# C v in smaller TensorE tiles, and a new order of the first loads, in a Nystrom attention and feed-forward kernel

## The chip, the cores and the metric

One core of one Trainium2 chip runs the whole kernel. The time is device microseconds of one execution, and the kernels are compared by the median of several executions. The core has a matrix engine (TensorE, PE in the profile, with its weight loads as PEld), a vector engine (DVE), a scalar engine (ACT), GpSimd (POOL) and a queue engine (SP) that issues DMAs. Each engine works through its own instructions in order; POOL and ACT issue some DMAs too.

## The reference

```python
def _attn_ref(q, k, v):                      # 8 batches, 8 heads, 576 rows, 64 columns, float32
    m, scale = 32, 1.0 / np.sqrt(D)
    q_lm = q.reshape(B, H, m, S // m, D).mean(axis=3)
    k_lm = k.reshape(B, H, m, S // m, D).mean(axis=3)
    A = sm(q, k_lm)                          # sm: row softmax of scale * a @ b.T
    Bm = sm(q_lm, k_lm)
    C = sm(q_lm, k)
    Z = Bm.T / (norm1(Bm) * norminf(Bm) + 1e-06)
    for _ in range(6):
        Z = 2 * Z - Z @ Bm @ Z
    return A @ Z @ C @ v

def _moe_ref(x, w1, w2, w3, w_out):          # x: 4608 x 512, the attention's heads side by side
    a = x @ w1                               # w1, w2: 512 x 1024
    b = x @ w2
    h = a * b @ w3                           # w3: 1024 x 1024
    return h @ w_out                         # w_out: 1024 x 512
```

## The kernel before

**How the work is cut.** Four heads of one batch are a quad; there are 16 quads, two to a batch. Two batches are a group, for which the 32x32 inverse is iterated at once; there are four groups. A batch's output is computed in three parts of 192 rows.

**Weights (L312 to L402).** `w3` and `w_out` are multiplied once, into `w34`, because nothing stands between the two products. `w3` comes in eight blocks of 128 rows (512 KB each, tiles `w3n`, a ring of three), is transposed on PE (`w3_tr`, L335), and split into a high and a low fp16 part by ACT (`w3_hi`, L342) and DVE (`w3_lo`, L349), half a block at a time. `w_out` comes in eight blocks (256 KB) and is split likewise (`wout_hi`, L321; `wout_lo`, L326). Each step `mm{j}{c}` is three matmuls of 512 columns. SP issues all of these loads (L309, L316); the first two blocks of `w3` come in two halves. `w_out` lands in the memory of the third and fourth `vb` tile.

**Attention of a quad (L646 to L706).** POOL issues the load of k and q (`lq`, L409), which turns them to fp16 on the way, into one of six `nat` tiles. DVE transposes them (`tk`, `tq`, L438). The means over 18 rows are made by POOL in three steps (`ma`, `mb`, `mc`, L446, L453, L461) for all quads but the first `NE` = 1, for which PE makes them (`M`, L471). PE then computes the scores with the landmarks (`S`, into the tile `wide`) and those of q (`A`); DVE finds maxima and differences (L514, L592, L598), ACT the exponentials (L541, L607), DVE the sums, POOL multiplies (`an`, L620), PE transposes (L629), ACT copies to `aT`.

**C v (L709 to L735).** The exponentials of C, transposed by DVE into `ecT` (L557), are the stationary operand in tiles of 128 rows by 32 columns. The two 64-row halves of a tile belong to two different heads. So that one product over 128 rows does both, each v tile `vb` holds 128 columns for a row, with zeros where row half and head don't match: `const_e` (L292) writes these zeros once on POOL, and a load of v (`load_v`, L414, four DMAs on SP) fills only the other blocks. The sums of the exponentials are masked the same way on POOL (`s_sums`, L546) and multiplied with `unit64`. For a batch this is 36 products of 128 columns and 4 of two columns, into one PSUM bank; DVE divides (`cv_out`, L731, L732).

**The inverse and the dense part.** `norm_mm`, `it_mm` (five rounds), `z_mm` and `w_mm` are small matmuls in 32x32 and 128x64 tiles (L764 to L849). Then, for each batch, `u_mm` (64x32 tiles, 512 columns) folds the inverse and C v into w1 and w2; `d1_mm` multiplies with `aT`; ACT (L954) and DVE (L960) make the product of the two branches, `ab`; `d2_mm` multiplies with `w34`; ACT scales (L986) and SP stores (L1001).

**What sets the order.** Every step is a task with an engine, an expected duration, dependencies, buffers that it takes (`acq`) and gives back (`rel`), a priority and an earliest start (`after`). `Plan.run` (L90) walks through them before the program is built and writes out a fixed order for each engine: of the tasks of an engine that can start soonest, the one with the lowest `prio`, where on PE a task in the tile mode that is set already has a bonus of `MP` = 1.2. The priorities come from `dense(b)` = 66 + 21 b, `att(n)`, `lane(g)` = `dense(2g)` - 16 and `cvt(b)` (L242 to L256). `SLACK` is added to every expected latency. The order that comes out is what each engine executes; nothing is reordered when a load comes late.

**Around the change.** POOL's first tasks are the identity (`cb`, L268), the zeros of the first two `vb` tiles (`ce0`), then the q/k loads; `ce1`, the zeros of the other two, waits for the last `wol` (the last use of `w_out`'s memory). The v loads of quads 0 to 3 wait for `ce0` or `ce1`. Six PSUM banks (`bank`) are shared by all steps.

Of the kernel before, what the change touches and what calls it, by code (L numbers as in the profile page):

```python
# [16 lines left out]
D = 64  # L17
# [3 lines left out]
NC9 = 9  # L21
# [3 lines left out]
MP = 1.2  # L25
# [15 lines left out]
class Plan:  # L41
# [6 lines left out]
    SLACK = 0.05  # L48
# [41 lines left out]
    def run(self):  # L90
# [15 lines left out]
        while len(order) < n:  # L106
            best = None
            for e, cand in avail.items():
                opts = []
                for t in cand:  # L110
                    found = self._slots(t.acq)
                    if found is None:
                        continue
                    at = max(free[e], t.ready, found[0], t.after)
                    opts.append((at, t, found[1]))
                if not opts:
                    continue
                first = min(o[0] for o in opts)
                near = [o for o in opts if o[0] <= first + (0.05 if e == "PE" else 0.0)]
                at, t, got = min(near, key=lambda o: (  # L120
                    o[1].prio - (MP if e == "PE" and o[1].mode == mode else 0.0)))
                if best is None or at < best[0]:
                    best = (at, t, got)
# [41 lines left out]
def kernel(  # L165
# [35 lines left out]
    vbs = slots(fixed, 4, [128, 2, 2, NC9, D], FP32, "vb")  # L201
# [26 lines left out]
    maskS = fixed.tile([128, 2], FP32, name="maskS")  # L228
# [13 lines left out]
    T0 = 66.0  # L242
    PER = 21.0
# [4 lines left out]
    def att(n):  # L248
        first = dense(2 * (n // 4)) - 42.0 + 7.0 * (n % 4)
        return max(0.0 + 6.0 * n, first)  # L250

    def lane(g):
        return dense(2 * g) - 16.0

    def cvt(b):
        return lane(b // 2) - 0.0 + 3.0 * (b % 2)  # L256

    NE = int(1.0)
    L0 = 9.0
    UO = 5.0  # L260
# [10 lines left out]
    def const_c():  # L271
        nc.vector.memset(blockones, 0.0)
        nc.vector.memset(ones, 1.0)
        nc.vector.memset(swapneg, 0.0)
        nc.vector.memset(maskS, 0.0)
        nc.vector.memset(meanS, 0.0)
        for s in range(2):
            nc.vector.memset(maskS[64 * s:64 * s + 64, s:s + 1], 1.0)
        for hh in range(4):
            r = slice(32 * hh, 32 * hh + 32)  # L280
            nc.vector.memset(meanS[r, hh:hh + 1], 1.0 / GRP)
            nc.vector.memset(blockones[r, r], 1.0)
        nc.vector.reduce_sum(out=iden32, in_=ident.rearrange("p (h x) -> p x h", h=4), axis=AX.X)
# [8 lines left out]
    def const_e(i):  # L292
        def fn():
            for t in vbs[2 * i:2 * i + 2]:
                for s in range(2):
                    nc.gpsimd.memset(t[64 * s:64 * s + 64, :, 1 - s, :, :], 0.0)
        return fn
# [5 lines left out]
    add("ce0", "POOL", 4.4, const_e(0), deps=["cb"], prio=-5.0)  # L303
    add("ce1", "POOL", 4.4, const_e(1), deps=[f"wol{c}" for c in range(8)], prio=24.0)
# [7 lines left out]
    def load_w3(j, n):  # L312
        def fn():
            for i in range(n):
                c = slice(DF // n * i, DF // n * i + DF // n)
                nc.sync.dma_start(out=w3n[at(f"w3n{j}")][:, c], in_=moe_w3[128 * j:128 * j + 128, c])  # L316
        return fn
# [12 lines left out]
    def w3_tr(j, h):  # L330
        def fn():
            ps = bank(at(f"ptr{j}{h}"))
            for i in range(4):
                c = 4 * h + i
                nc.tensor.transpose(out=ps[:, 128 * i:128 * i + 128],  # L335
                                    in_=w3n[at(f"w3n{j}")][:, 128 * c:128 * c + 128],
                                    identity=ident[:, :])
        return fn

    def w3_hi(j, h):  # L340
        def fn():
            nc.scalar.activation(out=w3t[at(f"w3t{j}")][:, 0, 512 * h:512 * h + 512],  # L342
                                 in_=bank(at(f"ptr{j}{h}")), func=AXF.Copy, scale=WSC)
        return fn

    def w3_lo(j, h):
        def fn():
            t = w3t[at(f"w3t{j}")]
            nc.vector.scalar_tensor_tensor(  # L349
                out=t[:, 1, 512 * h:512 * h + 512], in0=bank(at(f"ptr{j}{h}")), scalar=WSC,  # L350
                in1=t[:, 0, 512 * h:512 * h + 512], op0=ALU.mult, op1=ALU.subtract)
        return fn
# [17 lines left out]
    def w34_tasks():  # L370
        for j in range(8):
            p0 = 4.0 + 8.0 * j
            n = 2 if j < 2 else 1
            add(f"w3n{j}", "SP", 0.43 * n, load_w3(j, n), acq=[("w3n", f"w3n{j}", 1, 2)],
                prio=p0 - 8.0 if j > 1 else 0.115 * j, after=max(0.0, p0 - 12.0) if j > 1 else 0.0, move=1.46, lat=2.0)
# [8 lines left out]
            for h in range(2):  # L384
                acq = [("P", f"ptr{j}{h}", 1, 2)]
                if h == 0:
                    acq.append(("w3t", f"w3t{j}", 1, 8))
                add(f"tr{j}{h}", "PE", 0.44, w3_tr(j, h),
                    deps=["cb", f"w3n{j}"] + ([f"tr{j}0"] if h else []), acq=acq,
                    rel=[f"w3n{j}"], prio=p0 - 4.0 + h, mode="full")  # L390
                add(f"wh{j}{h}", "ACT", 0.48, w3_hi(j, h), deps=[f"tr{j}{h}"], rel=[f"ptr{j}{h}"],
                    prio=p0 - 3.5 + h)
                add(f"wl{j}{h}", "DVE", 0.61, w3_lo(j, h), deps=[f"tr{j}{h}", f"wh{j}{h}"],
                    rel=[f"ptr{j}{h}"], prio=p0 - 3.5 + h)
            for c in range(8):
                deps = [f"woh{c}", f"wol{c}", f"wh{j}{c // 4}", f"wl{j}{c // 4}"]
# [17 lines left out]
    def load_v(n):  # L414
        def fn():
# [3 lines left out]
            for s in range(2):  # L419
                for t in range(2):  # L420
                    p0 = 64 * s + 32 * t
                    nc.sync.dma_start(out=vb[p0:p0 + 32, :, s, :, :].rearrange("p a c d -> p a (c d)"),
# [123 lines left out]
    def s_sums(n):  # L546
        def fn():
            t = tinies[at(f"mx{n}")]
            nc.gpsimd.tensor_tensor(
                out=t[:, 8:12].rearrange("p (a s) -> p a s", a=2),  # L550
                in0=t[:, 4:6].unsqueeze(2).to_broadcast([128, 2, 2]),
                in1=maskS.unsqueeze(1).to_broadcast([128, 2, 2]), op=ALU.mult)
        return fn

# [91 lines left out]
    def quad_tasks(n):  # L646
        b, qd = divmod(n, 2)
        p = att(n)
        add(f"lq{n}", "POOL", 1.2, load_qk(n), acq=[("nat", f"nat{n}", 1, 3)],
            prio=p - (16.0 if n < 4 else 25.0),  # L650
            after=max(L0, p - (20.0 if n < 4 else 25.0)), move=3.3, lat=2.0)
        add(f"lv{n}", "SP", 1.75, load_v(n), acq=[("vb", f"vb{n}", 1, 1)], deps=[f"ce{n // 2}"] if n < 4 else [],
            prio=cvt(b) - 9.0 + qd, after=max(12.0, cvt(b) - 12.0 + 3 * qd), move=1.65, lat=2.0)
# [38 lines left out]
        add(f"ss{n}", "POOL", 0.2, s_sums(n), deps=[f"se{n}0", f"se{n}1"], prio=p + 2.0)  # L692
# [16 lines left out]
    def cv_mm(b):  # L709
        def fn():  # L710
            ps = bank(at(f"pC{b}"))
            for n in (2 * b, 2 * b + 1):
                qd = n % 2
                sums = tinies[at(f"mx{n}")][:, 8:12].rearrange("p (a s) -> p a s", a=2)
                for hp in range(2):
                    o = 32 * (2 * qd + hp)
                    mm(ps[o:o + 32, 128:130], unit64[:, :], sums[:, hp, :], pos=(0, o))
            for c in range(NC9):
                for n in (2 * b, 2 * b + 1):
                    qd = n % 2  # L720
                    for hp in range(2):
                        o = 32 * (2 * qd + hp)
                        mm(ps[o:o + 32, 0:128], ecTs[at(f"ecT{n}")][:, hp, c, :],
                           vbs[at(f"vb{n}")][:, hp, :, c, :], start=(c == 0), stop=(c == 8), pos=(0, o))
        return fn

    def cv_out(b):
        def fn():
            ps = bank(at(f"pC{b}"))
            rc = tinies[at(f"tc{b}")][:, 0:2]  # L730
            nc.vector.reciprocal(out=rc, in_=ps[:, 128:130])  # L731
            nc.vector.tensor_tensor(out=cvs[at(f"cv{b}")],  # L732
                                    in0=ps[:, 0:128].rearrange("p (s d) -> p s d", s=2),
                                    in1=rc.unsqueeze(2).to_broadcast([128, 2, D]), op=ALU.mult)
# [145 lines left out]
    def cv_tasks(b):  # L880
        n0, n1 = 2 * b, 2 * b + 1
        p = cvt(b)
        add(f"C{b}", "PE", 2.06, cv_mm(b),
            deps=[f"ct{n0}", f"ct{n1}", f"ss{n0}", f"ss{n1}"] + [f"lv{n0}", f"lv{n1}"],
            acq=[("P", f"pC{b}", 1, 1)], rel=[f"ecT{n0}", f"ecT{n1}", f"vb{n0}", f"vb{n1}", f"mx{n0}", f"mx{n1}"],
            prio=p, mode="128x32")
        add(f"co{b}", "DVE", 0.4, cv_out(b), deps=[f"C{b}"],
            acq=[("cv", f"cv{b}", 1, 1), ("tiny", f"tc{b}", 1, 1)],
            rel=[f"pC{b}", f"tc{b}"], prio=p + 2.0)
# [166 lines left out]
    P.ring("w3n", 3)  # L1056
# [5 lines left out]
    for s in range(2):  # L1062
        for qd in range(2):
            for wi in range(2):
                add(f"lw{s}{qd}{wi}", "POOL", 0.62, load_w12(s, qd, wi), prio=dense(0) - 22.0 + qd, after=dense(0) - 26.0,
                    move=0.75, lat=2.0)
# [12 lines left out]
    with tc.manual_schedule():  # L1079
        with tc.tile_pool(name="w34pool", bufs=1) as wp:  # L1080
            w3n = [obig[:, 2 * i:2 * i + 2, :].rearrange("p a x -> p (a x)") for i in range(2)]
            w3n.append(wp.tile([128, DF], FP32, name="w3n2"))
            wof = [vbs[2 + i // 4].rearrange("p a s c d -> p (a s c d)")[:, DM * (i % 4):DM * (i % 4) + DM]
                   for i in range(8)]
# [38 lines left out]
```

## Time and profile before

| | |
|---|---|
| median of 3 runs | 287.32 us (286.81 to 289.51) |
| the profiled execution | 290.63 us, its span 288.9 us |
| TensorE clock granted, mean | 0.992 |
| instructions on PE | 4098 matmuls and transposes, 4098 weight loads |
| DMA | 37.34 MB, mean 129 GB/s |

Busy time of the engines in stretches of the span, in us:

| stretch, us | PE | DVE | ACT | POOL | DMA share |
|---|---|---|---|---|---|
| 0 to 20 | 13.6 | 8.2 | 9.3 | 9.0 | 0.91 |
| 20 to 45 | 21.9 | 16.1 | 8.2 | 20.7 | 0.84 |
| 45 to 60 | 15.0 | 12.9 | 7.8 | 12.9 | 0.59 |
| 60 to 80 | 15.9 | 14.4 | 5.1 | 15.7 | 1.10 |
| 80 to 120 | 39.6 | 35.3 | 28.1 | 32.7 | 0.47 |
| 120 to 160 | 38.3 | 31.9 | 25.0 | 32.9 | 0.66 |
| 160 to 200 | 39.4 | 30.4 | 25.1 | 20.7 | 0.45 |
| 200 to 240 | 39.8 | 29.0 | 25.7 | 4.1 | 0.16 |
| 240 to 289 | 44.3 | 17.9 | 29.7 | 0.0 | 0.22 |

How the lines of the profile are read: in a group or a timeline line stand the line of the program, the engine, the operation, the tiles (out<-in, buffer numbers left out), and the partitions and elements of what is written and read; "x72" is how many there are. "<-" with an engine in a list of waits names what ended a wait; "issue" is time in which the engine waited for nothing that the profile shows. An fp32 matmul stands as two matmuls and two weight loads. All matmuls outside the transposes have the helper's line, L238, so their tiles tell them apart: `vb,ecT` is C v, `tiny,unit` its sums, `xz` the inverse, `bm` its norms, `wo,u` the product of `w3` and `w_out`, `w,wT` the u products, `aT,u` and `w,ab` the dense part, `Tk,lmT` the landmark scores.

### The profile page before, as it was taken

What the parts mean: (1) busy time and instruction counts of PE and PEld (TensorE: products, weight loads), DVE (VectorE), ACT (ScalarE), POOL (GpSimd) and SP (SyncE); (2) the same over time, 40 slices, a digit from 0 to 9 for tenths busy, and PEclk for the clock granted to TensorE, in tenths of its full rate; (3) what the DMA queues carried; (4) which work ended last, traced back from release to release, by engine and by line L of the source; (5) the groups of instructions that cost most, each with busy time, mean ns of one, the idle gap of its engine ahead of it and who ended that gap; (6) DMA issues with size and microseconds to landing.
All of it is one profiled execution on the core that took longest, in us unless ns stands there. A gap on an engine that the chain in (4) does not pass through costs nothing.

```text
span 288.9 us, 9979 instructions
## 1 busy us (share of the span) xinstructions
PE 267.8 (93%) x4098; PEld 176.8 (61%) x4098; DVE 196.0 (68%) x511; ACT 163.9 (57%) x456; POOL 148.9 (52%) x190
## 2 busy tenths in 40 slices
PE   3899699987899999989999999999999999999993
PEld 1446256655456767667667577667657775765762
DVE  0757549897468989956799798587958655443430
ACT  1743236424119798244967953478697454958551
POOL 8239688887897779999488789201111000000000
PEclk9999989999999999999999999999999999999999
DMA  6997982699950197601999816721212102111223
GB/s 196 302 313 183 258 203 75 108 205 263 254 128 2 21 182 148 129 7 39 217 241 217 198 48 178 184 83 40 73 39 76 39 13 68 57 54 52 98 74 109
DMA packets 19181, 37.34 MB, mean 129 GB/s; under 512 B 2880, under 2 KB 3136, under 8 KB 19136
## 3 DMA queue, kind: packets, MB, share of 16 engines
q1 hardware_dynamic: 13136, 24.91, 27.9%
q0 software_dynamic: 5760, 11.54, 23.2%
q8 instruction: 32, 0.52, 0.8%
q10 hardware_dynamic: 240, 0.26, 0.3%
q14 instruction: 13, 0.11, 0.1%
HBM read 38.80 MB, written 9.44 MB: 167 GB/s over the span
## 4 chain that ended last, share of the span: by engine, by line
PE 58%; DVE 18%; DMA 13%; ACT 5%; POOL 3%; issue 2%; SPq 0%; POOLq 0%; ACTq 0%; DVEq 0%
PE bank L238 53%; DMA nat<-in_q_dram 7%; DMA vb<-in_moe_w_out_dram 6%; DVE ab L960 4%; PE wide L238 2%; DVE bank L742 2%; DVE ea L598 2%; ACT u L876 2%; DVE tiny L613 2%; DVE tiny L592 1%; DVE tiny L514 1%; DVE ecT L557 1%; ACT ec L541 1%; POOL ls L453 1%; PE bank L629 1%
## 5 line engine op out<-in xcount | busy, mean ns | idle before, releaser
L238 PEld LDWEIGHTS <-u 128*128 128x128 f16 x960 | 81.4, 100 | 38.1 <-issue 9.4
L960 DVE TENSOR_TENSOR ab<-asb,bank 128x192 f16<-128x192 f16 x192 | 60.2, 346 | 31.7 <-ACT asb L954 30.7
L238 PE MATMUL bank<-aT,u 128*128 128x192 f16 x768 | 80.9, 246 | 0.0
L954 ACT CAST asb<-bank 128x192 f16<-128x192 f32 x192 | 59.0, 352 | 26.1 <-PE bank L238 23.5
L238 PE MATMUL bank<-w,ab 128*128 128x512 f16 (+1 forms) x296 | 73.2, 374 | 0.3
L238 PE MATMUL bank<-wo,u 128*128 128x512 f16 x192 | 52.2, 403 | 3.0 <-ACT u L342 2.6
L453 POOL TENSOR_TENSOR ls<-ls 128x128 f32<-128x128 f32 (+2 forms) x60 | 43.7, 729 | 4.3
L238 PEld LDWEIGHTS <-ab 128*128 128x128 f16 x296 | 27.0, 97 | 23.2 <-issue 5.1
L620 POOL TENSOR_TENSOR ah<-ea,tiny 128x512 f16<-128x512 f32 (+1 forms) x16 | 18.5, 1158 | 42.4 <-DVE tiny L534 24.7
L876 ACT CAST u<-bank 128x512 f16<-128x512 f32 x64 | 34.5, 611 | 5.8 <-PE bank L238 5.0
L446 POOL TENSOR_TENSOR ls<-nat 128x1152 f32<-128x1152 f16 x15 | 35.6, 2374 | 2.5 <-DMA nat<-in_q_dram 1.7
L986 ACT ACTIVATE osb<-bank 128x512 f32<-128x512 f32 x35 | 21.4, 613 | 13.6 <-PE bank L238 13.5
L541 ACT ACTIVATE ec<-wide,tiny 128x288 f32<-128x288 f32 x32 | 16.3, 524 | 6.4 <-DVE tiny L534 6.3
L238 PE MATMUL bank<-w,wT 64*32 64x512 f16 x512 | 19.3, 380 | 0.1
L238 PE MATMUL bank<-xz 32*32 32x64 f32 (+1 forms) x768 | 15.9, 213 | 2.9 <-issue 2.8
L461 POOL TENSOR_TENSOR lm<-ls,meanS 128x256 f16<-128x256 f32 x30 | 17.9, 618 | 0.7
L238 PEld LDWEIGHTS bank<-xz 32*32 32x32 f32 x768 | 11.6, 105 | 10.5 <-issue 5.2
L238 PE MATMUL bank<-vb,ecT 128*32 128x128 f32 x576 | 17.9, 273 | 0.0
L810 ACT COPY xz<-bank 128x128 f32<-128x128 f32 x16 | 4.3, 267 | 23.3 <-PE bank L238 18.9
L438 DVE STREAM_TRANSPOSE Tq<-nat 128x576 f32<-128x576 f32 x16 | 12.2, 762 | 7.4 <-DMA nat<-in_q_dram 7.4
L607 ACT ACTIVATE ea<-ea 128x512 f32<-128x512 f32 (+1 forms) x16 | 11.2, 703 | 9.4 <-DVE ea L598 9.4
L238 PEld LDWEIGHTS bank<-vb,ecT 128*32 128x32 f32 x576 | 15.8, 110 | 0.1
(91 smaller groups left out, 323.5 us busy)
## 6 DMA issues: line engine op xcount, KB each, us to landing
vb<-in_v_dram SPq DMA_DIRECT2D x64, 144.0 KB, 6.9
out_dram<-osb SPq DMA_DIRECT2D x37, 128.0 KB, 2.3
nat<-in_k_dram POOLq DMA_DIRECT2D x16, 288.0 KB, 6.1
nat<-in_q_dram POOLq DMA_DIRECT2D x16, 288.0 KB, 8.4
out_dram<-osb SPq DMA_DIRECT2D x16, 256.0 KB, 2.4
vb<-in_moe_w_out_dram SPq DMA_DIRECT2D x8, 256.0 KB, 7.6
osb<-in_moe_w_dram SPq DMA_DIRECT2D x4, 512.0 KB, 8.1
w<-in_moe_w_dram POOLq DMA_DIRECT2D x8, 256.0 KB, 7.3
```

What stands on the lines that cost most here:

```text
L238: nc.tensor.matmul(out_, lhsT, rhs, start=start, stop=stop, **({} if pos is None else {"tile_position": pos}))
L438: nc.vector.transpose(out=T.rearrange("p r l e -> p (r l e)").bitcast(FP32), in_=nats[at(f"nat{n}")][:, t].rearrange("p r d -> p (r d)").b ...
L446: nc.gpsimd.tensor_tensor(out=l, in0=nat[:, :, 0:9, :], in1=nat[:, :, 9:18, :], op=ALU.add)
L453: nc.gpsimd.tensor_tensor(out=l[:, :, x:x + m, :], in0=l[:, :, x:x + m, :], in1=l[:, :, y:y + m, :], op=ALU.add)
L461: nc.gpsimd.tensor_tensor(out=lm[:, 4 * t:4 * t + 4, :], in0=l[:, t, 0, :].unsqueeze(1).to_broadcast([128, 4, D]), in1=meanS.unsqueeze(2). ...
L541: nc.scalar.activation(out=ecs[at(f"ec{n}")][:, hp, :, :].rearrange("p c x -> p (c x)"), in_=psS[:, hp, 0:HALF], func=AXF.Exp, scale=SCALE ...
L607: nc.scalar.activation(out=ea, in_=ea, func=AXF.Exp, scale=SCALE)
L620: nc.gpsimd.tensor_tensor(out=ahs[at(f"ah{n}")][:, 0:g, :], in0=eas[at(f"ea{n}")][:, 0:g, :], in1=tinies[at(f"ta{n}")][:, 0:g].unsqueeze(2 ...
L876: nc.scalar.copy(out=uu[at(f"u{b}{qd}")][:, wi, 512 * half:512 * half + 512], in_=bank(at(f"pU{b}{wi}{half}{qd}")))
L954: nc.scalar.copy(out=asb[at(f"as{b}{j}{th}")], in_=bank(at(f"pD{b}{j}{th}"))[:, 0:THIRD])
L960: nc.vector.tensor_mul(ab[:, j, c0:c0 + THIRD], asb[at(f"as{b}{j}{th}")], bank(at(f"pD{b}{j}{th}"))[:, THIRD:2 * THIRD])
L986: nc.scalar.activation(out=osb[at(f"os{t}")], in_=bank(at(f"pE{t}")), func=AXF.Copy, scale=2.0 ** -12)
```

## The change

C v is computed in tiles of 64 rows by 32 columns, each row half on its own with the 64 columns of its head, and each half into a PSUM bank of its own: 72 products of 64 columns and 8 of one column for a batch, for 36 of 128 and 4 of two. The zero blocks, their memsets, the mask and the masked sums go. A v tile is half as large and there are six for four. The output is divided half by half.

The first `w3` block comes in three parts (128, 384 and 512 columns), the parts between the first `w_out` blocks; all other blocks come whole. There are four `w3n` tiles for three. `w_out` lands in the memory of the `ecT` tiles and of two `u` tiles.

A small copy on POOL reads the second `w_out` block; every q/k load depends on it (task `gt`).

The priorities and earliest starts move: `dense(b)` is 62 + 20 b, `att` of the first four quads goes from 24, 31, 38, 45 to 11, 17.5, 24, 30.5, `lane` is `dense` - 22 for - 16, `cvt` is `lane` - 4 for `lane`; the bonus for the same tile mode is 0.6 in full mode and 1.0 in tile modes; the means of two quads (`NE` = 2) are made on PE.

```diff
-MP = 1.2
+MP = 0.6
+MT = 1.0
-    SLACK = 0.05
+    SLACK = 0.1
-                    o[1].prio - (MP if e == "PE" and o[1].mode == mode else 0.0)))
+                    o[1].prio - ((MP if mode == "full" else MT) if e == "PE" and o[1].mode == mode else 0.0)))
-    vbs = slots(fixed, 4, [128, 2, 2, NC9, D], FP32, "vb")
+    vbs = slots(fixed, 6, [128, 2, NC9, D], FP32, "vb")
-    T0 = 66.0
-    PER = 21.0
+    T0 = 62.0
+    PER = 20.0
-        first = dense(2 * (n // 4)) - 42.0 + 7.0 * (n % 4)
-        return max(0.0 + 6.0 * n, first)
+        first = dense(2 * (n // 4)) - 51.0 + 6.5 * (n % 4)
+        return max(3.0 + 6.0 * n, first)
-        return dense(2 * g) - 16.0
+        return dense(2 * g) - 22.0
-        return lane(b // 2) - 0.0 + 3.0 * (b % 2)
-    NE = int(1.0)
+        return lane(b // 2) - 4.0 + 3.0 * (b % 2)
+    NE = int(2.0)
-    UO = 5.0
+    UO = 4.0
...
-    add("ce0", "POOL", 4.4, const_e(0), deps=["cb"], prio=-5.0)
-    add("ce1", "POOL", 4.4, const_e(1), deps=[f"wol{c}" for c in range(8)], prio=24.0)
+    GATE = int(1.0)
+    def gate():
+        nc.gpsimd.tensor_copy(out=gates, in_=wof[at(f"wf{GATE}")][:, 0:1])
+    add("gt", "POOL", 0.15, gate, deps=[f"wf{GATE}"], prio=-8.0)
...
-            n = 2 if j < 2 else 1
-            add(f"w3n{j}", "SP", 0.43 * n, load_w3(j, n), acq=[("w3n", f"w3n{j}", 1, 2)],
-                prio=p0 - 8.0 if j > 1 else 0.115 * j, after=max(0.0, p0 - 12.0) if j > 1 else 0.0, move=1.46, lat=2.0)
+            cuts = [(0, 1), (1, 4), (4, 8)] if j == 0 else [(0, 4), (4, 8)]
+            acq = [("w3n", f"w3n{j}", 1, len(cuts))]
+            if j == 0:
+                for h, (c0, c1) in enumerate(cuts):
+                    add(f"wm{h}" if h else "w3n0", "SP", 0.43, load_w3(0, 128 * c0, 128 * c1),
+                        acq=[] if h else acq, prio=(-0.01, 0.105, 0.115)[h], move=0.183 * (c1 - c0), lat=2.0)
+            else:
+                add(f"w3n{j}", "SP", 0.43, load_w3(j), acq=acq, prio=0.125 if j == 1 else p0 - 8.0,
+                    after=0.0 if j == 1 else max(0.0, p0 - 12.0), move=1.46, lat=2.0)
...
-        add(f"lq{n}", "POOL", 1.2, load_qk(n), acq=[("nat", f"nat{n}", 1, 3)],
-            prio=p - (16.0 if n < 4 else 25.0),
-            after=max(L0, p - (20.0 if n < 4 else 25.0)), move=3.3, lat=2.0)
+        add(f"lq{n}", "POOL", 1.2, load_qk(n), deps=["gt"], acq=[("nat", f"nat{n}", 1, 3)],
+            prio=p - (16.0 if n < 4 else 23.0),
+            after=max(L0, p - (20.0 if n < 4 else 23.0)), move=3.3, lat=2.0)
...
-        add(f"ss{n}", "POOL", 0.2, s_sums(n), deps=[f"se{n}0", f"se{n}1"], prio=p + 2.0)
...
+            ps = [bank(at(f"pC{b}{s}")) for s in range(2)]
+            for c in range(-1, NC9):
                 for n in (2 * b, 2 * b + 1):
                     for hp in range(2):
+                        o = 32 * (2 * (n % 2) + hp)
+                        for s in range(2):
+                            r = slice(64 * s, 64 * s + 64)
+                            if c < 0:
+                                mm(ps[s][o:o + 32, 64:65], unit64[r, :], tinies[at(f"mx{n}")][r, 4 + hp:5 + hp],
+                                   pos=(64 * s, o))
+                            else:
+                                mm(ps[s][o:o + 32, 0:64], ecTs[at(f"ecT{n}")][r, hp, c, :],
+                                   vbs[at(f"vb{n}")][r, hp, c, :], start=(c == 0), stop=(c == 8),
+                                   pos=(64 * s, o))
...
+            for s in range(2):
+                ps = bank(at(f"pC{b}{s}"))
+                rc = tinies[at(f"tc{b}")][:, s:s + 1]
+                nc.vector.reciprocal(out=rc, in_=ps[:, 64:65])
+                nc.vector.tensor_scalar(out=cvs[at(f"cv{b}")][:, s, :], in0=ps[:, 0:64], scalar1=rc,
+                                        scalar2=None, op0=ALU.mult)
...
-    P.ring("w3n", 3)
+    P.ring("w3n", 4)
...
-                add(f"lw{s}{qd}{wi}", "POOL", 0.62, load_w12(s, qd, wi), prio=dense(0) - 22.0 + qd, after=dense(0) - 26.0,
-                    move=0.75, lat=2.0)
+                add(f"lw{s}{qd}{wi}", "POOL", 0.62, load_w12(s, qd, wi), prio=T0 - 19.0 + qd, after=T0 - 19.0 - 4.0,
+                    move=1.46, lat=2.0)
...
+            w3n += [wp.tile([128, DF], FP32, name=f"w3n{i}") for i in (2, 3)]
+            wof = [ecTs[i].rearrange("p a c x -> p (a c x)")[:, 0:DM] for i in range(4)]
+            wof += [uu[i // 2][:, i % 2, :].bitcast(FP32) for i in range(4)]
```

## The prediction

> **What bounds the kernel now.** I read the page first, then the list of waits of the matrix engine, then its timeline around those waits, then busy time by windows.
>
> ```profile
> PE 267.8 (93%) x4098; PEld 176.8 (61%) x4098; DVE 196.0 (68%) x511; ACT 163.9 (57%) x456; POOL 148.9 (52%) x190
> q8 instruction: 32, 0.52, 0.8%
> PE 58%; DVE 18%; DMA 13%; ACT 5%; POOL 3%; issue 2%; SPq 0%; POOLq 0%; ACTq 0%; DVEq 0%
> ```
>
> PE is busy for 267.8 of 288.9 us, and no other engine comes near. So what counts is PE's own work and the 21.1 us in which it stands; 4.6 of these are the last store and 3.6 the first load. Its waits (total us, times, longest us):
>
> ```profile
> PE bank L335 <- DMA osb<-in_moe_w_dram: 3.6, 1, 3.6
> PE bank L238 <- ACT ec L541: 2.9, 1, 2.9
> PE bank L238 <- issue: 2.8, 3, 1.6
> PE wide L238 <- DVE tiny L514: 2.8, 1, 2.8
> PE bank L238 <- ACT u L342: 2.6, 1, 2.6
> ```
>
> All are early, but for the last of the three "issue" waits, in which PE waits for nothing that the profile shows. The timeline puts the first of those right behind a C v block:
>
> ```profile
> 70.22 0.24 PE L238 MATMUL bank<-tiny,unit 128*32 128x2 f32 x8
> 70.30 2.15 PE L238 MATMUL bank<-vb,ecT 128*32 128x128 f32 x72
> 72.38 0.29 PE L238 MATMUL bank<-xz 32*32 32x64 f32 x2
> 73.58 0.64 PE L238 MATMUL bank<-xz 32*32 32x64 f32 x30 [0.90 <-issue]
> ```
>
> The next one ends at 79.77, the third at 124.07. By windows (length; busy us and instructions of PE, PEld, DVE, ACT, POOL; clock, DMA share, GB/s):
>
> ```profile
> 31.86:34.65 2.79, 0.00 (x1) 0.01 (x1) 2.67 (x6) 0.63 (x1) 2.36 (x1) 1.00 1.05 255
> 34.90:38.30 3.40, 3.40 (x11) 1.17 (x11) 2.46 (x6) 1.07 (x4) 1.50 (x3) 0.50 1.10 260
> 73.57:79.76 6.19, 5.87 (x128) 3.04 (x128) 3.25 (x7) 1.40 (x4) 4.84 (x5) 1.00 1.10 252
> 118.36:124.06 5.70, 3.94 (x128) 3.02 (x126) 4.51 (x16) 0.68 (x2) 5.30 (x7) 1.00 0.66 146
> ```
>
> Between two "issue" waits lie exactly 128+128 instructions, and the page shows 32 packets of the instruction queue for 4098+4098 instructions: 256 in each. PE reads its program in pages of 256, the next page is asked for when one is entered, and here a page could not be left before 6.19 and 5.70 us, with the DMA engines 1.10 and 0.66 busy. This decides the case, since the change doubles the instructions of C v.
>
> **C v in 64x32 tiles.** One block (a batch) lasts from 70.22 to 72.38, 2.16 us; eight make 17.3. Each of the new tiles streams 64 columns in place of 128, and eight tiles stand where four did: half, 1.08 us, is the lower bound. That eight 64x32 tiles run side by side in fp16 is shown by the u products, 32 matmuls of 512 columns in 1.06 us where one lasts 0.39: (1.06-0.39)/3 = 0.22 for each eight. In fp32 the nearest row is the last product of the inverse, 32 pairs of weight load and matmul from 83.36 to 83.75, 12 ns a pair with the change of tile mode; 72x2+16 = 160 pairs at that pace take 1.9. I take 1.3, near the lower end, as the stream bound is from C v itself. Gain 0.86 x 8 = 6.9 us (8.6 to 2.1), all on PE and so on the path.
>
> **Its instruction pages.** A block issues 320 instructions in place of 160: every block crosses a page, and a quarter cross two. Let a page not be left before L us after it was entered. If x of 256 were gone when C v starts, at 0.03 us each (windows 80 to 120 us: 1369 in 40 us), and the rest go at 1.3/320 = 0.004, the stall is L - 0.03x - 0.004(256-x). Averaged over x, with a second stall of L-1.05 where x is over 192, a block loses 0.8 us at L=3, 1.4 at 4, 2.2 at 5, 3.1 at 6. L is about 6 where loads are dense (above); after 124 us no such wait is listed, though pages pass in 4 us. I take 5 for the two blocks of group 0, 4 for group 1, 3 for the last two groups: 2x(2.2+1.4+0.8+0.8) = 10.4, less the 2.8 that stand in the waits already: +7.6 (0 to +18.5). So C v returns what it saves. The Trainium skill (Runtime: NRT & Kernel Launch, Instruction fetch mechanics) says that fetching is hidden behind dispatch, with 2048 instructions held for the matrix engine; by it this term would be 0. The waits at multiples of 256 disagree.
>
> **Zero blocks, masks, sums.** GpSimd loses eight memsets of 1.05 us and 16 masked sums of 0.21. The memsets are on the path once, as the chain of waits shows (start, us, what):
>
> ```profile
> 20.39 1.02 POOL vb L296
> 21.46 1.05 POOL vb L296
> 22.52 0.47 POOL nat L409
> 22.99 8.96 DMA nat<-in_q_dram
> 31.98 0.78 DVE Tq L438
> ```
>
> The last memsets waited for w_out (POOL waits 10.3 us for L326), held the third q/k load to 22.5, and VectorE, in order, stood 3.5 us at its transpose; PE stood from 31.86 to 34.65 and then ran 3.4 us at clock 0.50, which loses 1.7 more. In the new order this load follows the second without a memset, some 14 us sooner. Gain 2.8+1.7 = 4.5 at most; transfers and order shift too, so I take 3.6 (4.5 to 0). Two PSUM banks instead of one for 1.3 us eight times: nothing while four others serve the dense products; 0.35 us (one DVE product) each if not. C v's output becomes four DVE instructions, 2x(0.15+0.22) for 0.15+0.29, +0.3 x 8 = 2.4 on an engine 68% busy, hidden by PE's backlog; on the path at worst 2.4.
>
> **w3, the gate, order.** The first w3 part is 64 KB for 256, so the first w_out block has 320 KB with it for 768. At the 0.7 us per 256 KB at which w_out landed, that is 1.2 us sooner than its use at 7.38; it feeds PE's 2.6 us wait. The gate on POOL waits for the second w_out block (before: 8.07); behind it are only the q/k issues, which stood behind memsets until 5.60. Their packets began only after 9.5 us (8 in the first ten), so q/k data come about 1 us later and w_out has the engines that much longer. The v loads lose their wait for memsets but keep their place behind w3 on SP, where a fourth w3 buffer shortens L316's waits for PE (11.4 us): 0. The tiles that now take w_out are first written again at 36.76 (ecT), long after its last use at 20.3: 0. Whole w3 blocks: one issue for two on SP, 0.35 to 0.45 us, hidden; three conversions for two on ACT and DVE, 0.2 each, hidden by w_out's arrival. Together -2.0 (-4 to +2, the same wait moved to VectorE's first transposes). Quad 1's means move from POOL (2.37+3.14+1.19) to PE: 18 matmuls, 1.17 us on the path, +1.2. Earlier priorities, the rings and the mode bonus move work, remove none; the 2.9 us wait for ACT may stay, go or double: 0 (-2.9 to +2.9).
>
> **Sum.** -6.9 + 7.6 - 3.6 - 2.0 + 1.2 = -3.7 us. The profiled run took 290.63 with a span of 288.9, 3.3 over the median of 287.32; the same difference from the median gives 283.6.
>
> **Rivals.** *Pages cost nothing*, because C v is placed where a page has just been read or the fetch keeps up: -11.3, 276.0. For it: no issue wait after 124 us. Against: three at page ends.
>
> *Pages bind* (slower): L is 6 in groups 0 to 2, whose loads are no fewer, and 4 in the last: 2x(3x3.1+1.4) = 21.4, less 2.8, +18.6; with the other terms +7.3, 294.6. It decides from 1.8 us a block, L of about 4.6. For it: 6.19 and 5.70 measured. Against: quiet pages of 4 us.
>
> *Small matmuls go one at a time*: eight of 32 columns in the score products start at 84.77 and the next kind at 84.97, 25 ns each. At that, C v takes 160x0.025 = 4.0 us, +14.7; pages then hardly matter, and 297.7 comes out. The score products' sixteen of 288 columns, 0.46 us where one lasts 0.29, come 11 ns apart, the inverse's 12; both speak against. The Trainium skill (TensorE: Matmul & The Clock Gate, "Wait - 56ns, not 53.3ns?") states a floor of about 25 ns from start to start however small the matmul. The inverse's 12 ns disagree for separate tiles.
>
> *The start gains nothing*: VectorE stands at transposes of quads whose loads, all earlier now, share the engines with w_out. Then -6.9+7.6+1.2, 289.2.
>
> **Chances.** Forecast 0.44 (own range 279 to 287), pages free 0.19, pages bind 0.22, one at a time 0.04, start 0.11. One per cent, 2.9 us, is about what a measurement of this kernel tells from none. Faster: two thirds of the forecast and pages free, 0.48. Same: the rest of the forecast and most of the start case, 0.23. Slower: 0.29. The range 275 to 293 leaves out half of the pages-bind case, the one-at-a-time case and the tail of pages free, 0.2.
>
> **What would show it.** C v blocks of about 1.3 us between start and next kind, apart from "issue" waits; those waits grown from 2.8 to about 10 us, at instruction counts 256 apart, most in the first two groups; no PE gap near 32 us and no clock of 0.50 after the first 15 us; the third q load landed by 24 us. C v at 2 us or more, issue waits under 4 or over 15, or VectorE standing for q/k loads before 40 us would make the prediction wrong.

## The result and the profile after

| | before | after |
|---|---|---|
| median, on one chip | 288.41 us (286.81 to 290.97, 4 runs) | 298.96 us (296.45 to 299.6, 4 runs) |
| the profiled execution, its span | 290.63 us, 288.9 us | 299.6 us, 297.6 us |
| PE busy, PE idle in the span | 267.8 us, 21.1 us | 270.9 us, 26.7 us |
| mean granted clock of TensorE | 0.992 | 0.973 |

The ratio after to before is 1.0341, with a 95% interval of 1.0237 to 1.0445. The change made the kernel slower by 3.4%; the forecast was 1.3% faster.

The page of the changed kernel: busy time by engine, the instruction queue's packets, the chain of waits.

```profile
PE 270.9 (91%) x4756; PEld 180.4 (61%) x4756; DVE 197.8 (66%) x527; ACT 168.2 (57%) x457; POOL 131.1 (44%) x160
q8 instruction: 37, 0.61, 0.9%
PE 70%; DMA 11%; issue 6%; POOL 5%; DVE 5%; ACT 1%; SPq 0%; ACTq 0%; POOLq 0%
```

PE issues 658 more matmuls and as many weight loads, in five more pages of its program. It is busy for longer, not for less, and "issue" has gone from 2% of the chain to 6%. The list of PE's waits (total us, times, longest us):

```profile
PE bank L239 <- issue: 12.8, 7, 4.3
PE bank L327 <- DMA osb<-in_moe_w_dram: 5.9, 4, 2.9
PE wide L239 <- DVE lmT L484: 2.2, 1, 2.2
PE bank L239 <- ACT w L358: 0.5, 1, 0.5
PE bank L239 <- ACT u L865: 0.2, 1, 0.2
```

Waits for nothing that the profile shows grew from 2.8 us to 12.8. Of the other early waits, those for `ec` (2.9), `u` (2.6, now 0.2) and `tiny` (2.8) went; w3's grew from 3.6 to 5.9, and one for the landmarks, 2.2 us, is new. The timeline of PE around the longest "issue" wait shows where it sits:

```profile
61.30 0.22 PE L239 MATMUL bank<-tiny,unit 64*32 64x1 f32 x2
...
62.12 1.98 PE L239 MATMUL bank<-vb,ecT 64*32 64x64 f32 x143
64.03 0.42 PE L239 MATMUL bank<-bm,ones 32*32 32x128 f32 x8
64.27 0.30 PE L239 MATMUL bank<-bm 32*32 32x32 f32 x15
68.91 0.34 PE L239 MATMUL bank<-bm 32*32 32x32 f32 x17 [4.35 <-issue]
```

The inverse's 32 norm matmuls are cut in two after the fifteenth, by 4.35 us. C v ran just ahead, and ate its page. A C v block that meets no stall, again PE's timeline:

```profile
42.60 0.27 PE L239 MATMUL bank<-tiny,unit 64*32 64x1 f32 x16
42.72 1.90 PE L239 MATMUL bank<-vb,ecT 64*32 64x64 f32 x144
44.55 1.47 PE L239 MATMUL bank<-wo,u 128*128 128x512 f16 x6
```

From 42.60 to 44.55 is 1.95 us for 160 pairs of weight load and matmul, 12 ns a pair. The eight blocks, with the waits inside them taken out, are 1.80 to 2.09 us long, 15.5 in all; before they took 18.05. Windows of the same run (length; busy us and instructions of PE, PEld, DVE, ACT, POOL; clock, DMA share, GB/s) show what a stall leaves behind it:

```profile
64.56:68.91 4.35, 0.00 (x1) 0.00 (x1) 0.45 (x3) 0.00 (x0) 4.12 (x3) 1.00 1.11 208
217.12:219.32 2.20, 0.00 (x1) 0.00 (x0) 0.00 (x0) 0.00 (x0) 0.00 (x0) 1.00 0.00 0
69.80:73.20 3.40, 3.40 (x11) 1.55 (x9) 2.01 (x7) 1.19 (x2) 2.01 (x4) 0.50 0.41 80
100.59:103.99 3.40, 3.40 (x22) 3.13 (x22) 1.55 (x5) 1.59 (x5) 3.39 (x4) 0.51 0.96 152
220.00:223.40 3.40, 3.40 (x40) 2.09 (x23) 2.68 (x8) 1.88 (x4) 0.00 (x0) 0.50 0.02 5
```

Each of the three longest "issue" waits is followed within 0.9 us by 3.4 us in which PE runs without a break at half the clock. If that work goes by the clock, 1.7 us of it take 3.4, a loss of 1.7 each (an estimate). The second row is worth a second look: while PE stood there no other engine worked, and no DMA packet began; the packet of the instruction queue that had begun at 216.69 ran until 217.95.

**Where 8.7 us of span came from.** Idle time, +5.6: "issue" +10.0, w3 +2.3, the landmarks +2.2, less 2.9 (`ec`), 2.4 (`u`) and 2.8 (`tiny`), and some 0.8 less in smaller waits. Busy time, +3.1: clock halves +5.1 (four stretches of 3.4 us ahead of the last stores for one), means +1.2, C v -2.6, and 0.6 less in overlaps. The clock's share is that of this execution: the other three had mean clocks of 0.984 to 0.988, so less of it, and their spans were only 0.3 to 3.1 us shorter.

**All stalls are page ends.** The count takes in all that the trace holds of PE: matmuls, weight loads, and 42 instructions that wait for semaphores or drain the engine. In it every one of the seven stalls comes after exactly 193 + 256 k instructions, as the three of before did. (Matmuls and weight loads alone give distances that are a few short of multiples of 256.) Around them the trace gives the instruction queue's packets too:

| page entered, us | its 256 instructions gone | the next page's packet, from and to | DMA share until then | PE goes on | after the packet |
|---|---|---|---|---|---|
| 62.78 | 64.37 | 66.39 to 67.47 | 1.14 | 68.91 | 1.44 |
| 95.64 | 98.12 | 98.25 to 99.19 | 0.92 | 100.59 | 1.40 |
| 117.39 | 119.30 | 119.01 to 119.96 | 0.45 | 121.28 | 1.32 |
| 127.34 | 132.15 | 130.78 to 131.77 | 1.08 | 133.33 | 1.56 |
| 173.99 | 176.83 | 175.20 to 176.53 | 1.01 | 178.12 | 1.59 |
| 215.52 | 216.91 | 216.69 to 217.95 | 0.61 | 219.32 | 1.37 |
| 227.16 | 228.94 | 227.16 to 228.13 | 0.03 | 229.47 | 1.34 |

(The DMA share is that of the window from the page's entry to the packet's start; in the last row, where the two coincide, of the window 226.16 to 228.13.)

A page entered is not left before its successor has been read: pairing pages and packets in order, at all 36 such changes of this trace, with a stall or without, the next page begins at least 1.32 us after its packet's end. In the stalled pages entering to leaving took from 2.3 us (0.97 for the packet, 1.34 after it) to 6.1, where the packet itself began 3.6 us late, with the DMA engines full. Six of the seven pages have C v in them and are gone in 1.4 to 2.9 us; the one entered at 127.34 has none, is gone in 4.8, and met a packet that began 3.4 us late.

### The profile page after: what moved, and what is told of

It reads as the page before. It is cut to its first block, busy times and chain, and to the rows that moved or that the text cites. A ratio compares the mean times of both kernels' runs of the same rounds, so it can differ in the third digit from the quotient of the medians.

```text
span 297.6 us, 11265 instructions
## 1 busy us (share of the span) xinstructions
PE 270.9 (91%) x4756; PEld 180.4 (61%) x4756; DVE 197.8 (66%) x527; ACT 168.2 (57%) x457; POOL 131.1 (44%) x160
## 4 chain that ended last, share of the span: by engine, by line
PE 70%; DMA 11%; issue 6%; POOL 5%; DVE 5%; ACT 1%; SPq 0%; ACTq 0%; POOLq 0%
PE bank L239 65%; DMA nat<-in_q_dram 9%; PE wide L239 3%; POOL ls L453 2%; DMA ecT<-in_moe_w_out_dram 2%; POOL nat L409 1%; PE bank L620 1%; POOL ls L446 1%; DVE bank L731 1%; POOL ah L611 1%; PE bank L327 1%; DVE tiny L604 1%; DVE Tk L438 0%; DVE Tq L438 0%; DVE tiny L514 0%
## 5 line engine op out<-in xcount | busy, mean ns | idle before, releaser
L239 PEld LDWEIGHTS <-u 128*128 128x128 f16 x960 | 83.5, 101 | 35.8 <-issue 11.6
L239 PE MATMUL bank<-wo,u 128*128 128x512 f16 x192 | 53.1, 409 | 0.0
L865 ACT CAST u<-bank 128x512 f16<-128x512 f32 x64 | 35.0, 595 | 15.7 <-PE bank L239 15.5
L453 POOL TENSOR_TENSOR ls<-ls 128x128 f32<-128x128 f32 (+2 forms) x56 | 40.8, 728 | 3.8
L446 POOL TENSOR_TENSOR ls<-nat 128x1152 f32<-128x1152 f16 x14 | 33.3, 2379 | 15.9 <-DMA nat<-in_q_dram 15.5
L334 ACT ACTIVATE u<-bank 128x512 f16<-128x512 f32 (+2 forms) x17 | 9.7, 571 | 21.7 <-PE bank L327 21.7
L239 PE MATMUL bank<-vb,ecT 64*32 64x64 f32 x1152 | 16.1, 225 | 2.5 <-issue 2.5
L461 POOL TENSOR_TENSOR lm<-ls,meanS 128x256 f16<-128x256 f32 x28 | 16.7, 618 | 0.5
L239 PEld LDWEIGHTS bank<-vb,ecT 64*32 64x32 f32 x1152 | 14.4, 105 | 3.1 <-issue 2.8
L239 PE MATMUL bank<-xz 32*32 32x64 f32 (+1 forms) x768 | 15.1, 213 | 1.0 <-issue 1.0
```

What stands on the lines that cost most here:

```text
L239: nc.tensor.matmul(out_, lhsT, rhs, start=start, stop=stop, **({} if pos is None else {"tile_position": pos}))
L446: nc.gpsimd.tensor_tensor(out=l, in0=nat[:, :, 0:9, :], in1=nat[:, :, 9:18, :], op=ALU.add)
L453: nc.gpsimd.tensor_tensor(out=l[:, :, x:x + m, :], in0=l[:, :, x:x + m, :], in1=l[:, :, y:y + m, :], op=ALU.add)
L461: nc.gpsimd.tensor_tensor(out=lm[:, 4 * t:4 * t + 4, :], in0=l[:, t, 0, :].unsqueeze(1).to_broadcast([128, 4, D]), in1=meanS.unsqueeze(2). ...
L865: nc.scalar.copy(out=uu[at(f"u{b}{qd}")][:, wi, 512 * half:512 * half + 512], in_=bank(at(f"pU{b}{wi}{half}{qd}")))
```

## The experiments

The theory after the result: the doubled instructions of C v use up pages faster than they can be read, and the stalls halve the clock; C v itself is bound by the pace of issue, and the rest of the change is a small gain. The rivals: C v is bound by the columns that it streams; the new order, the loads or the gate cost the time; the stalls belong to the traffic and not to C v.

### The halves of the change, each alone

The changed kernel with the old C v:

```diff
-    vbs = slots(fixed, 6, [128, 2, NC9, D], FP32, "vb")
+    vbs = slots(fixed, 4, [128, 2, 2, NC9, D], FP32, "vb")
+    add("ce0", "POOL", 4.4, const_e(0), deps=["cb"], prio=-8.5)
+    add("ce1", "POOL", 4.4, const_e(1), deps=["cb", "lq3"], prio=-8.0)
...
-        add(f"C{b}", "PE", 1.3, cv_mm(b), deps=[f"ct{n0}", f"ct{n1}", f"lv{n0}", f"lv{n1}"],
+        add(f"C{b}", "PE", 2.06, cv_mm(b),
```

> The changed kernel with the C v of before (128x32 tiles, zero blocks, masked sums; the memsets of the first two v tiles ahead of the gate, those of the other two behind the fourth q/k load), everything else of the change kept. Theory pages: the loss is the 10 us by which the issue waits grew (12.8 for 2.8) and three halved clocks of 3.4 us behind them (5.1), against 2.6 us that C v's blocks themselves got shorter: issue waits back under 5 us, clock 0.99, about 299.0 - 10 - 5.1 + 2.6 = 286.5, between 283 and 290. Rival start: the new order of loads and priorities is what costs; then the time stays at 294 or more, with issue waits small.

It took 283.05 us (281.17 to 285.51) where before took 288.28 on that chip, ratio 0.9862 (0.9672 to 1.0053), so that the gain over before is not clear of noise in this run; the gain over the changed kernel is. PE's waits:

```profile
PE bank L340 <- DMA osb<-in_moe_w_dram: 6.0, 4, 2.9
...
PE bank L240 <- issue: 0.2, 1, 0.2
```

The "issue" waits are gone, the granted clock is 1.000 on average, and the w3 wait of 6.0 us is there without the new C v: it belongs to the loads. Against the changed kernel's trace the new C v thus costs 17.2 us of span: "issue" waits 12.6, halved clocks 6.8, the landmarks' wait 1.7, less 2.2 in C v's own blocks, the rest -1.7.

The kernel before with the new products alone (zero blocks and masks stay, unused):

```diff
+            ps = [bank(at(f"pC{b}{s}")) for s in range(2)]
+            for c in range(-1, NC9):
...
+                                   vbs[at(f"vb{n}")][r, hp, s, c, :], start=(c == 0), stop=(c == 8),
```

> The kernel before with only the products of C v and their division in the new form; zero blocks, memsets, masked sums (written, no longer read) and all loads and priorities stay. Theory pages: issue waits of 10 to 20 us at instruction counts 256 apart, halved clocks behind the long ones, C v blocks of 1.9 us without the waits: 295 to 304. Rival start: 288.4 less 2.6, between 284 and 288.

It took 310.93 us, ratio 1.0854 (1.0748 to 1.0961), more than either theory had said. PE's waits:

```profile
PE bank L238 <- issue: 16.9, 8, 5.3
...
PE bank L629 <- issue: 1.8, 1, 1.8
```

Against before, the span grew by 20.3: "issue" 15.9 and halved clocks 8.5 (stretches at 69.9 and 189.3, each 6.8 us long, and at 124.5 and 240.5), less 2.0 in C v's blocks and 2.1 in other waits and overlaps. The old order puts two C v blocks side by side at 183, and stalls come within them, 2.2 and 3.0 us.

### Fewer instructions in a row

C v cut into five tasks, whose priorities are 2 us apart, so that the planner sets other products between them:

```diff
+        cuts = [-1, 2, 4, 6, 8, NC9]
+        for i in range(5):
...
+                prio=p + 2.0 * i, mode="64x32")
```

> The changed kernel with each C v block cut into five tasks of 16 or 8 products, two units of priority apart, so that other matmuls come between; the same products. A page then takes about 5 us. Theory pages: issue waits under 5 us, no halved clock after 60 us, 299 - 9 - 5 + 3 for some 30 more changes of tile mode = 288, between 284 and 291. Rival start: 296 or more. Rival pace (a pair each 12 ns is what costs, wherever it stands): within 1 per cent of 299.

294.26 us, ratio 1.0264 (1.0156 to 1.0372). "Issue" waits fell from 12.8 to 6.3 us, the longest to 3.2, and one stretch of halved clock is left of four. The runs (293.72 to 294.36, one of 299.32) lie below the changed kernel's but for that one. The instructions are the same in number, which speaks for their density as the cause; but the new order also moved the work against the page ends, and this run can't part the two. The time fell by less than expected, as half of the waits stayed and one of 2.4 us for `ah` came in.

### The page boundary moved

Sixteen fp32 matmuls of one column in front of w3's first transposes put every later instruction 64 places further into its page:

```diff
+PADS = 16
...
+                for _ in range(PADS):
+                    mm(ps[0:32, 0:1], ident[:, 0:32], ident[:, 0:1], pos=(0, 0))
```

> The changed kernel with 16 fp32 matmuls of one column ahead of the first transpose, 64 instructions, about 1 us of work at the start, so that all page ends move by 64 instructions against the work and nothing else does. Theory pages: page ends fall into nine blocks of small matmuls instead of seven; from the changed kernel's instruction times and a page time falling from 6 us at the start to 3 at the end, the waits sum to 19 to 24 us against 15 so computed for the changed kernel (13.4 measured): issue waits of 16 to 22 us, still at counts 256 apart, the first in the C v block of batch 0 at about 45 us, where there was none; 303 to 311. Rival: waits belong to places in the program and not to counts, and stay where they were: 299 to 301.

305.62 us, ratio 1.0635 (1.0471 to 1.0798). The waits, then PE's timeline at the first C v block, which had no stall in the changed kernel:

```profile
PE bank L240 <- issue: 19.4, 8, 6.5
```

```profile
42.59 0.27 PE L240 MATMUL bank<-tiny,unit 64*32 64x1 f32 x16
42.72 1.88 PE L240 MATMUL bank<-vb,ecT 64*32 64x64 f32 x142
51.05 0.42 PE L240 MATMUL bank<-vb,ecT 64*32 64x64 f32 x2 [6.45 <-issue]
```

The block begins at the same 42.59, and is cut two of its matmul records before its end. Data, loads and order are those of the changed kernel, but for the added work at the start; the count moved, and the stalls followed it to 193 + 256 k. So a page end is what stalls, and where it falls is worth some 5 to 7 us by itself (the spans of the profiled executions are 302.2 and 297.6, the medians 305.62 and 298.96).

### Instructions or columns

Half of v's columns left out of C v's products (32 of 64; the other half of C v is not computed), with as many instructions:

```diff
-                                mm(ps[s][o:o + 32, 0:64], ecTs[at(f"ecT{n}")][r, hp, c, :],
-                                   vbs[at(f"vb{n}")][r, hp, c, :], start=(c == 0), stop=(c == 8),
+                                mm(ps[s][o:o + 32, 0:32], ecTs[at(f"ecT{n}")][r, hp, c, :],
+                                   vbs[at(f"vb{n}")][r, hp, c, 0:32], start=(c == 0), stop=(c == 8),
```

> The changed kernel with 32 of the 64 columns in each C v product; the other half of v is left out, so C v is only half computed. As many instructions, half the streaming. Theory pace (a pair of weight load and matmul each 12 ns is what a block lasts, not its columns): blocks stay at 1.8 to 2.0 us without waits, issue waits at 11 to 15 us, 295 to 303. Theory stream (columns set the time): blocks of about 1.0 us.

302.45 us in one run, no less than the changed kernel; its "issue" waits sum to 15.9 us. PE's timeline at the first block:

```profile
43.14 0.27 PE L239 MATMUL bank<-tiny,unit 64*32 64x1 f32 x16
43.27 1.70 PE L239 MATMUL bank<-vb,ecT 64*32 64x32 f32 x144
44.90 1.47 PE L239 MATMUL bank<-wo,u 128*128 128x512 f16 x6
```

1.76 us for 1.95: half the columns save a tenth. The pace is that of the instructions, 11 ns a pair.

The counterpart keeps tiles, columns and places, and nearly halves the instructions: C v's operands in fp16, which the trace shows as one matmul and one weight load for two of each. ACT turns v to fp16 in tiles of its own (`vf` is where it lands):

```diff
-    vbs = slots(fixed, 6, [128, 2, NC9, D], FP32, "vb")
-    ecTs = slots(fixed, 4, [128, 2, NC9, M], FP32, "ecT")
+    vbs = slots(fixed, 6, [128, 2, NC9, D], FP16, "vb")
+    vfs = slots(fixed, 3, [128, 2, NC9, D], FP32, "vf")
+    ecTs = slots(fixed, 4, [128, 2, NC9, M], FP16, "ecT")
...
+        add(f"lc{n}", "ACT", 1.05, cast_v(n), deps=[f"lv{n}"], acq=[("vb", f"vb{n}", 1, 1)], rel=[f"vf{n}"], prio=cvt(b) - 2.0 + qd)
```

> The changed kernel with C v's two operands in fp16 (ACT writes the exponentials so, and turns v from a landing tile), same tiles, same places; an fp16 product takes one weight load and one matmul where fp32 takes two: 176 instructions a block in place of 320. Theory pages: blocks of about 1.1 us, issue waits of 2 to 6 us, at most one halved clock: 283.1 for the changed kernel with old C v, less 8 x 1.1, plus 5: 280, between 275 and 286. Rival: small tiles or two banks cost as such, whatever the type: 292 or more.

283.13 us (282.71 to 283.52), ratio 0.9811 (0.9705 to 0.9917). Its PE waits, in full down to 1.2 us:

```profile
PE bank L328 <- DMA osb<-in_moe_w_dram: 6.9, 4, 2.9
PE bank L240 <- DVE ab L955: 3.0, 5, 1.0
PE bank L626 <- POOL ah L617: 1.7, 1, 1.7
PE wide L240 <- DVE lmT L490: 1.5, 1, 1.5
PE bank L240 <- DVE bank L757: 1.2, 2, 0.9
```

No "issue" wait stands in it, the blocks take 0.70 to 0.82 us but for one of 1.0 that overlaps other work, the page shows 32 packets of the instruction queue again, and one halved stretch is left, at 50.7, behind the landmarks' wait. With fewer instructions, 72 + 16 pairs a block for 160, the small tiles and the two banks cost nothing that shows. But it is no faster than the changed kernel with the old C v in fp32 (283.05): against that trace PE is busy for 6.0 us less (259.8 for 265.8) and idle for 7.1 more (21.7 for 14.6), so what the blocks save comes back as waits.

The same in the old tiles (the changed kernel with the old C v, in fp16) looked better still:

> The changed kernel with the old 128x32 tiles and zero blocks in C v, operands in fp16 as in after_hA (ACT turns v in two pieces, about 2 us a quad): 88 instructions a block. Theory pages and pace: blocks of 0.5 to 0.7 us, issue waits under 2 us, clock above 0.99: 283.1 - 8 x 1.6 = 270, between 267 and 277. Rival: ACT, with 33 us more, holds up u or the dense part and gives it back: 280 or more.

It took 291.3 us, ratio 1.011 (1.0013 to 1.0208). Most blocks fell to 0.70 us, but v needs two conversions on ACT for one, because of the zero blocks, and ACT's busy time went from 167.5 to 199.8 us. PE's waits:

```profile
PE bank L650 <- DVE ab L981: 5.0, 4, 2.0
PE bank L241 <- DVE ab L981: 2.5, 3, 1.8
```

`ab` is made from what ACT copies. The time is the rival's (280 or more), and the new waits for what ACT feeds fit its reason, that the engine that was given the conversions is late; no run gave them to another engine.

### What the rest of the change is worth

In the kernel before, `w_out` lands elsewhere (as in the changed kernel), and the last zeros wait for the third q/k load instead of for `w_out`:

```diff
-    add("ce1", "POOL", 4.4, const_e(1), deps=[f"wol{c}" for c in range(8)], prio=24.0)
+    add("ce1", "POOL", 4.4, const_e(1), deps=["cb", "lq2"], prio=-4.0)
```

> The kernel before, with w_out landing in the ecT and u tiles as in the change, and the memsets of the third and fourth v tile no longer waiting for w_out but queued behind the third q/k load; nothing else. Theory of the prediction: the third q load lands before 26 us instead of 31.95, PE's wait of 2.8 us near 32 us and the halved clock behind it go: 288.3 - 3.6, between 283.5 and 286. Rival: the same wait comes back at another load, and the time stays within 1 per cent of 288.3.

292.4 us, ratio 1.0138 (1.005 to 1.0226): no gain. The third q load landed by 20.99 instead of 31.95, and the stall near 32 us and its halved clock are gone; but PE's waits now hold a longer one, with 6.8 us of halved clock at 68.7:

```profile
PE bank L629 <- POOL ah L620: 4.2, 1, 4.2
```

From the changed kernel with the old C v, first the gate alone was taken out (the q/k loads no longer wait for the second `w_out` block), then, with the gate and the loads of w3 and `w_out` kept, all priorities, earliest starts, the bonus, the slack and the means of the second quad were put back (the q/k, w1 and w2 loads take their old places with them, and the last zeros stand behind the second q/k load for the fourth):

```diff
-    add("gt", "POOL", 0.15, gate, deps=[f"wf{GATE}"], prio=-8.0)
```

> This is the changed kernel with the old C v (zero blocks, 36 products of 128 columns a batch), which took 283.05 us, without the task that makes the q/k loads wait for the second w_out block. If that wait is what the new start gains, the q/k packets share the engines with w_out again, PE waits 1 to 4 us more for w_out in the first 15 us, and the time is 284 to 288. If the wait is worth nothing (the third q/k load is early either way, as no memset stands ahead of it), the time is 281 to 285 and the first two q loads land 1 to 2 us sooner.

282.77 us, ratio 0.9841 (0.9743 to 0.994): the gate is worth nothing that shows.

```diff
-    T0 = 62.0
-    PER = 20.0
+    T0 = 66.0
+    PER = 21.0
...
-    NE = int(2.0)
+    NE = int(1.0)
```

> The changed kernel with the old C v, and besides it with the old priorities, earliest starts, mode bonus, slack and the means of one quad on PE; the new loads, the wait for w_out, the ring of four w3 tiles and the place of w_out stay. If the priorities carry what that kernel gained (283.05 against 288.28), it takes 286 to 292. If loads and places carry it, 282 to 285.

289.56 us, ratio 1.0037 (0.9995 to 1.0079): the gain is gone. PE's waits are those of a poor early order, and the clock is halved at 34.5 and 68.7:

```profile
PE bank L240 <- DVE xz L831: 3.4, 2, 2.1
PE bank L642 <- POOL ah L633: 2.8, 1, 2.8
PE wide L240 <- DVE tiny L527: 1.9, 1, 1.9
```

So what the changed kernel gained outside C v needs the new order; the new loads with the old order brought none of it. A new order without the new loads was not run.

### Could the fp16 version be better still

The planner is told 0.8 us for C v in place of 1.3:

> The changed kernel with C v's operands in fp16 (283.13 us, blocks of 0.70 to 0.82 us, no issue waits), where the planner reckons 0.8 us for a block instead of 1.3. If the order suffers from the wrong duration, 278 to 282; if not, 282 to 285, with the waits for w3 (about 7 us) where they are.

284.68 us, ratio 0.9878 (0.981 to 0.9945). And with it, the means of four quads on PE for two:

> As the last, with the means of four quads made on PE for two: 36 more fp32 matmuls, 2.3 us more on PE, and some 13 us less on GpSimd in the first 45 us. If the early waits for DVE and GpSimd cost more than that, 276 to 282 (waits for ab and ah gone); if PE's own work decides and no page wait comes back, 283 to 287.

285.21 us, ratio 0.9887 (0.9804 to 0.9969). Neither differs from 0.9811 by more than the intervals. In the first, three "issue" waits (3.0 us) and one of 4.7 for `ea` appear; in the second, a wait for `ah` of 3.8 and a halved clock of 6.8 us at 59.0. Moving work by a microsecond or two brings new early waits that cost what it saves. Both intervals lie below 1, but neither version is shown to be better than the changed kernel with C v in fp16 (0.9811) or, without lower precision, the changed kernel with the old C v and no gate (0.9841).

## Why the prediction was wrong

The forecast was -3.7 us against the profiled run; the spans differ by +8.7, 12.4 us more. By its terms:

- **C v, the step that failed: "I take 1.3, near the lower end, as the stream bound is from C v itself. Gain 0.86 x 8 = 6.9 us."** Measured: 1.80 to 2.09 us a block, a gain of 2.6. The upper end, 1.9 at the inverse's 12 ns a pair, was right and was turned down. The old block's pairs took 27 ns each with 128 columns (2.17 us for 80), the new ones 12 with 64, and 11 with 32: from 64 columns down it is no longer the columns that set the time, so half the columns did not mean half the time. This is 4.3 us of the error.
- **Instruction pages, +7.6: mechanism right, size short.** "Issue" waits rose by 10.0, in the forecast's own "about 10 us" and at counts 256 apart. With little more than half of C v's instructions none was left (3.0 us in another order), and a shift by 64 took them to 19.4. The times L of 5, 4 and 3 us were of the right size (6.1, 5.0 and 3.9 until 121 us, 6.0 and 4.1 in the pages entered at 127 and 174, 3.8 and 2.3 in the last group). 2.4 us of the error.
- **What a stall does to the clock was left out of this term.** The profile of before showed it (2.79 us of standing, then 3.4 us at 0.50), and the forecast counted it as a gain where a stall went, but not as a loss where stalls came. Three page stalls cost 3 x 1.7 = 5.1 us in the profiled execution, the largest piece of the error there; in the kernel before with the new products alone the clock cost 8.5.
- **The start, -3.6 - 2.0: near in sum, wrong in cause.** With the old C v the change gained some 5 us, as the terms say with the +1.2 of the means (-4.4); that the sum came near is luck. Moving the memsets alone gained nothing (ratio 1.0138), the gate is worth nothing, and with the old priorities the gain is gone. The term that was put at 0, "earlier priorities ... move work, remove none", is the one that it could not do without. In the changed kernel the third q load landed at 26.70, 5.2 us sooner than before but not by 24, and the stall near 32 us moved to 46, where PE waits 2.2 us for the landmarks and then runs 3.4 at half clock: these 1.7 us were not gained.
- **The banks, VectorE's divisions, the means:** as forecast. No PE wait of note goes back to a bank of C v, VectorE's busy time rose by 1.8 us for 2.4, and the second quad's 18 matmuls took 1.17.
- **The rivals.** "Pages bind" had the sign and, with 294.6, a time nearer to 298.96 than the forecast, but by 21.4 us of page stalls and C v at 1.3 us, and neither was so. "Small matmuls one at a time" came nearest of all, with 297.7, but from 4.0 us a block, wrong by two. The sentence that makes a forecast wrong in its own words, "C v at 2 us or more", is almost what was measured.
- **The rule on fetching.** The Trainium skill (Runtime: NRT & Kernel Launch, Instruction fetch mechanics) lets this kernel's pages cost nothing. With the other terms of the forecast that would have given 276.0, and this case shows 12.8 us of stalls at page ends, one of them (from 217.12) while no other engine had work.

What stays open: whether it is the traffic that delays a page's packet. The table's rows fit that in the main (3.6, 3.4 and 2.6 us at DMA shares of 1.14, 1.08 and 0.92, but 1.2 at 1.01; 1.6 and 1.2 at 0.45 and 0.61, none at 0.03). Over all pages of the changed kernel's trace, every packet that began more than 2 us after its page was entered (up to 5.2) did so at a share of 0.9 or more, and none at a share under 0.1 began later than 1.2. But no run changed the traffic alone. Which of the priorities carries the gain of the order was not tried either.

## What to carry to other kernels

Before a product is cut into smaller tiles, count the instructions: here a tile that streams half the columns gained little once its weight load and matmul took their 12 ns, and dense runs of short instructions used up the program faster than it was read. Look for waits that nothing in the profile releases, check whether they lie a constant number of instructions apart, and price each with the clock that it leaves behind. Here a type that needs half the instructions, or other work between the small matmuls, took back all or part of the loss; but the old, larger tiles in fp32 did as well (283.05 against 283.13).

## What was unexpected of the hardware

- A page of 256 instructions of TensorE could not be left before 2.3 us even with the DMA engines at 0.03: 0.9 to 1.3 us for the packet, and 1.3 to 1.6 us more before PE went on in the seven stalls.
- After a stall of 2.2 us on an otherwise quiet core, the clock was 0.50 for 3.4 us (220.0 to 223.4): no other engine had run during the pause, so PE's own standing was enough. The changed kernel's shorter page stalls, up to 1.8 us, left none; but with the new products in the kernel before one of 1.80 us left a halved stretch (from 124.5), and with half the columns one of 1.79 (from 122.7).
- Where a page end falls by chance is worth microseconds: 64 instructions more at the start, some 0.4 us at 12 ns a pair, took the "issue" waits from 12.8 to 19.4.
